# Feed-forward products turned round, and the last part's eight block products replaced by seven

## The chip, the cores and the metric

The kernel runs on one core of a Trainium2 chip. The metric is the device time of one execution in microseconds (us); the median of three runs before is 516.29 us (516.12 to 516.65).

## What is computed

The program has three stages. Banded attention with a few global keys and a distance bias (4 batches, 8 heads, 768 positions, head width 64) gives x of 3,072 tokens by 512. A soft mixture of eight experts with 32 slots follows. Its output, still 3,072 by 512, goes through a dense feed-forward layer, which is what the change touches:

```
h = x @ w_in            # (3072 x 512) @ (512 x 2048)
r = np.maximum(h, 0.0)
g = r * r
return g @ w_out        # (3072 x 2048) @ (2048 x 512)
```

All inputs arrive as 64-bit numbers, or in words from which the kernel makes 32-bit floats itself.

## The kernel before

Every engine runs its instructions in the order in which the program issues them: the schedule is written by hand. The kernel's first part (attention, routing, experts) ends near 220 us in the profile. Since the mixture's output is a product of rank 32 (combine weights `cst` times slot outputs), w_in is first multiplied by the slot outputs into a small matrix `U`, so that one matmul of depth 128 gives h for 128 features and 512 tokens (`gemm1`, L1017).

The 2,048 features are cut into five parts, `WIDTHS` (L32). For each part q and each chunk d of 512 tokens, `gemm1` makes J = width/128 tiles of h. `gate` (L1006) turns each into g: ScalarE (ACT) takes the ReLU out of PSUM (L1008), VectorE (DVE) makes the square in full precision (L1009), ACT the square rounded to the format that TensorE multiplies quickly (L1010), and GpSimd (POOL) the remainder, full minus rounded (L1011; in part 0 DVE does it). w_out is split in the same way into a rounded part `hi` and a remainder `lo` (`conv_out`, L961).

`gemm2` (L1031) takes 128 tokens at a time: g's tile is the stationary operand, 512 columns of w_out the moving one, and for each of the J tiles there are three products, hi by hi, hi by lo, lo by hi (L1042 to L1044), summed in one PSUM bank (tag `acc`, 3 banks). In part 0 ACT copies the bank to the running sum `oacc` (L1049), in the others DVE adds it (L1051); in the last part the sum then goes out by DMA from the SP queue. The very last 128 tokens are done in two halves of 256 columns, the second DMA going from ACT's queue (L1054 to L1061).

The main loop (L1139 to L1154) runs over parts and chunks. `gemm1` and `gate` run one chunk ahead of `gemm2`; the tiles of g have two buffers. Beside them, spread over the first five of the six chunks of a part, `background` (L1129) prepares the next part: it loads the words, converts them to floats (`convert`, L926: one ACT and three DVE operations for 512 columns), makes U (`make_u`, L977) and splits w_out (L971 on ACT, L972 on POOL).

Of the kernel before, what the change touches and what calls it, by code (L numbers as in the profile page):

```python
# [39 lines left out]
def attention_moe_ffn(ctx: ExitStack, tc, qk, vx, nn, phi, w1, w2, w_in, w_out, consts, relw, out):  # L40
    nc = tc.nc
    V, G = nc.vector, nc.gpsimd
# [17 lines left out]
    acc = full("acc", [P, DM])  # L60
# [135 lines left out]
    def slot(tag, shape, dt, name):  # L196
        return (pre if tag[0] == "p" else stream).tile(shape, dt, tag=tag, name=name)
# [752 lines left out]
    def conv_in(q):  # L950
        W = WIDTHS[q]
        if q:
            f = slot("p4", [P, 4, W], F32, f"winf{q}").rearrange("p a c -> p (a c)")
        else:
            f = hZ[:, E * HS : E * HS + 4 * W]
        wq[q] = {"f": f.rearrange("p (a c) -> p a c", c=W)}
        for c0 in range(0, 4 * W, 512):
            yield from convert(raw[q][0], c0, f[:, c0 : c0 + 512], f"i{q}")
            yield

    def conv_out(q):  # L961
        J = WIDTHS[q] // P
        t = slot(("s1", "p6")[q % 2], [P, 4096], F32R, f"w{q}")
        w = t[:, 0 : 2 * J * DM].rearrange("p (a j c) -> p a j c", a=2, c=DM)
        hi, lo = w[:, 0, :, :], w[:, 1, :, :]
# [65 lines left out]
    def gemm2(q, k):  # L1031
        g2 = g_of(q, k // 4)
        ghi, glo = g2[:, 0, :, :], g2[:, 1, :, :]
        whi, wlo = wq[q]["hi"], wq[q]["lo"]
        pa = fps.tile([P, 512], F32, tag="acc", name=f"acc{q}_{k}", bufs=3)
        ms = slice(k % 4 * P, k % 4 * P + P)
        J = WIDTHS[q] // P
        o = oacc[k // 4][:, k % 4, :]

        def products(cs):  # L1040
            for j in range(J):
                nc.tensor.matmul(pa[:, cs], lhsT=ghi[:, j, ms], rhs=whi[:, j, cs], start=j == 0, stop=False)  # L1042
                nc.tensor.matmul(pa[:, cs], lhsT=ghi[:, j, ms], rhs=wlo[:, j, cs], start=False, stop=False)  # L1043
                nc.tensor.matmul(pa[:, cs], lhsT=glo[:, j, ms], rhs=whi[:, j, cs], start=False, stop=j == J - 1)  # L1044

        if k < NT // P - 1 or q < len(WIDTHS) - 1:
            products(slice(0, DM))
            if q == 0:
                nc.scalar.copy(o, pa)  # L1049
            else:  # L1050
                V.tensor_tensor(o, pa, o, op=ALU.add)  # L1051
            if q == len(WIDTHS) - 1:
                nc.sync.dma_start(out[k * P : k * P + P, :], o)
        else:  # L1054
            for c, eng in ((0, nc.sync), (TB, nc.scalar)):
                cs = slice(c, c + TB)
                if c:
                    pa = fps.tile([P, 512], F32, tag="acc", name=f"acc{q}_{k}_2", bufs=3)
                products(cs)
                V.tensor_tensor(o[:, cs], pa[:, cs], o[:, cs], op=ALU.add)  # L1060
                eng.dma_start(out[k * P : k * P + P, cs], o[:, cs])  # L1061
# [256 lines left out]
```

## Time and profile before

| | before |
|---|---|
| median of 3 runs | 516.29 us |
| the profiled execution | 516.84 us |
| its span, first to last instruction | 515.0 us |
| PE busy | 507.0 us (98%) |
| PE weight loads busy | 387.7 us (75%) |
| DVE busy | 379.5 us (74%) |
| ACT busy | 306.4 us (59%) |
| POOL busy | 142.2 us (28%) |
| granted TensorE clock | 1.00 |

PE is TensorE's matmuls. Their recorded times overlap, because matmuls are pipelined; what a matmul costs in a packed stretch is the distance from its start to the next start. The feed-forward products run from about 221 us to the end.

### The profile page before, as it was taken

How to read it: one execution, taken by the hardware profiler on the slowest of the kernel's cores; microseconds unless marked ns; L12 is line 12 of the kernel's file. 1: busy time of each engine (PE TensorE's matmuls, PEld its weight loads, DVE VectorE, ACT ScalarE, POOL GpSimd, SP SyncE). 2: the span in 40 equal slices, each digit the busy share in tenths (PEclk: the TensorE clock that was granted, in tenths of full speed). 3: DMA queues.
4: the chain of work that ended last, by engine and by line, in shares of the span. 5: the costliest groups of instructions: out<-in, count | busy, mean ns of one | idle time of the engine just before them, and what ended most of it. 6: DMA issues, size and time to landing. Idle time of an engine off the chain costs nothing.

```text
span 515.0 us, 9799 instructions
## 1 busy us (share of the span) xinstructions
PE 507.0 (98%) x3532; PEld 387.7 (75%) x3532; DVE 379.5 (74%) x925; ACT 306.4 (59%) x804; POOL 142.2 (28%) x125
## 2 busy tenths in 40 slices
PE   9999999999999999999999999999999999999997
PEld 6777777677767744477887878878888788888886
DVE  7788878787888836688799986968746668445552
ACT  6977877787888302397965555555544455433440
POOL 7000000000000110001443675436744436534450
PEclk9999999999999999999999999999999999999999
DMA  8789989999994899904404040200300000002333
GB/s 285 255 291 301 352 308 329 325 328 301 317 326 153 266 371 423 404 13 165 163 1 163 1 164 1 104 19 1 122 2 0 1 0 3 0 14 110 122 123 122
DMA packets 25975, 86.93 MB, mean 169 GB/s; under 512 B 2882, under 2 KB 5442, under 8 KB 23746
## 3 DMA queue, kind: packets, MB, share of 16 engines
q1 hardware_dynamic: 25776, 86.13, 46.8%
q8 instruction: 29, 0.48, 0.4%
q14 instruction: 24, 0.20, 0.1%
q10 hardware_dynamic: 146, 0.13, 0.1%
HBM read 79.95 MB, written 6.29 MB: 167 GB/s over the span
## 4 chain that ended last, share of the span: by engine, by line
PE 58%; DVE 3%; POOL 0%; issue 0%; ACT 0%; POOLq 0%; DVEq 0%
PE acc L1044 16%; PE acc L1042 16%; PE acc L1043 16%; PE h L1017 4%; PE pSO L922 3%; DVE cvyo L933 1%; PE pu L982 1%; PE pre L818 1%; DVE rg L1009 1%; DVE cvyo L936 1%; DVE cvyo L932 1%; DVE oacc_p L1051 0%; PE pc L883 0%; PE pu L1112 0%; PE sel L912 0%; PE pu L990 0%
## 5 line engine op out<-in xcount | busy, mean ns | idle before, releaser
L1044 PE MATMUL acc<-w,g 128*128 128x512 f32 (+1 forms) x387 | 150.3, 388 | 1.1 <-POOL g L1011 1.1
L1042 PE MATMUL acc<-w,g 128*128 128x512 f32 (+1 forms) x387 | 150.1, 388 | 0.0
L1043 PE MATMUL acc<-w,g 128*128 128x512 f32 (+1 forms) x387 | 150.0, 388 | 0.0
L1011 POOL TENSOR_TENSOR g<-rg,g 128x512 fp32r<-128x512 f32 x84 | 109.0, 1300 | 126.5 <-DVE rg L1009 82.4
L1008 ACT ACTIVATE rg<-h 128x512 f32<-128x512 f32 (+1 forms) x97 | 57.6, 593 | 90.7 <-PE h L1017 84.7
L262 ACT ACTIVATE sm<-sm,nm 128x256 f32<-128x256 f32 (+1 forms) x192 | 92.7, 487 | 1.2 <-DVE nm L247 1.2
L1044 PEld LDWEIGHTS acc<-w,g 128*128 128x128 f32 x387 | 72.7, 188 | 16.8 <-POOL g L1011 1.5
L1042 PEld LDWEIGHTS acc<-w,g 128*128 128x128 f32 x387 | 72.7, 188 | 15.1 <-ACT oacc_p L1049 0.2
L1043 PEld LDWEIGHTS acc<-w,g 128*128 128x128 f32 x387 | 72.7, 188 | 14.9
L1009 DVE SCALAR_TENSOR_TENSOR rg<-h,rg 128x512 f32<-128x512 f32 (+1 forms) x97 | 66.1, 681 | 14.0 <-ACT rg L1008 13.7
L1051 DVE TENSOR_TENSOR oacc_p<-acc,oacc_p 128x512 f32<-128x512 f32 x63 | 43.3, 688 | 44.5 <-PE acc L1044 44.4
L247 DVE CUSTOM_DVE_ANT_0 sm<-s,mask 128x256 f32<-128x256 f32 (+1 forms) x192 | 66.8, 396 | 2.0 <-ACT sm L262 1.2
L1010 ACT ACTIVATE g<-rg 128x512 fp32r<-128x512 f32 (+1 forms) x97 | 61.0, 629 | 3.1
L234 PE MATMUL s<-raw 64*128 64x256 f32 (+1 forms) x384 | 52.8, 397 | 0.0
L273 PE MATMUL pt<-con,sm 128*128 128x128 f32 x352 | 45.4, 276 | 1.6 <-ACT pT L279 1.6
L672 POOL TENSOR_TENSOR lh<-lh 128x256 f32<-128x256 f32 x1 | 0.7, 731 | 158.2 <-PE pt L273 158.2
L290 PE MATMUL o<-pT,v 128*64 128x128 f32 x704 | 44.2, 276 | 0.0
L273 PEld LDWEIGHTS pt<-con,sm 128*128 128x128 f32 x352 | 38.5, 141 | 7.2 <-ACT pT L279 2.8
L234 PEld LDWEIGHTS s<-raw 64*128 64x128 f32 x384 | 32.1, 194 | 14.7 <-DMA v<-in_vx 6.5
L290 PEld LDWEIGHTS o<-pT,v 128*64 128x64 f32 x704 | 37.9, 137 | 6.9 <-ACT sm L262 2.1
L1017 PE MATMUL h<-cu 128*128 128x512 f32 x94 | 37.1, 394 | 0.0
L262 ACT ACTIVATION_READ_ACCUMULATOR sm<-sm,nm 128x1 f32 x192 | 36.9, 192 | 0.0
(222 smaller groups left out, 549.2 us busy)
## 6 DMA issues: line engine op xcount, KB each, us to landing
w<-in_w SPq DMA_DIRECT2D x40, 512.0 KB, 6.6
raw<-in_qk SPq DMA_DIRECT2D x32, 384.0 KB, 4.8
w<-in_w SPq DMA_DIRECT2D x5, 2048.0 KB, 9.2
v<-in_vx SPq DMA_DIRECT2D x32, 256.0 KB, 4.0
raw<-in_qk SPq DMA_DIRECT2D x16, 320.0 KB, 5.0
win<-in_w_in SPq DMA_DIRECT2D x2, 2048.0 KB, 7.9
wout<-in_w_out SPq DMA_DIRECT2D x2, 2048.0 KB, 8.0
out_x<-oacc_p SPq DMA_DIRECT2D x15, 256.0 KB, 2.0
```

Of the source, the lines that this page charges most:

```text
L234: nc.tensor.matmul(sc[hh][:, tt, 0:n, :], lhsT=r[r0 : r0 + D, tt, :], rhs=rhs, start=True, stop=True)
L247: V.tensor_tensor_reduce(out=sm[:, j, 0:n, :], in0=sc[hh][:, tt, 0:n, :], in1=m[:, 2:3, :] if n == 1 else m[:, 0:2, :], scale=-QK_SCALE, s ...
L262: nc.scalar.activation(sm[:, j, 0:n, :], sm[:, j, 0:n, :], AF.Exp, bias=nm[:, j : j + 1], scale=-1.0, accum_out=chunk_sums(i // NPR)[:, tt ...
L273: nc.tensor.transpose(pp[tt][:, hh, c, :], sm[:, 2 * tt + hh, c, :], ident)
L290: nc.tensor.matmul(o[hh * D : hh * D + D, tt, :], lhsT=v[:, c * 3 if tt == 0 else 1 + c, hh * D : hh * D + D], rhs=pT[:, 2 * tt + hh, c, : ...
L1009: V.scalar_tensor_tensor(g, ph, 0.0, r, op0=ALU.max, op1=ALU.mult)
L1010: nc.scalar.activation(g2[:, 0, js, cs], r, AF.Square)
L1011: (G if q else V).tensor_tensor(g2[:, 1, js, cs], g, g2[:, 0, js, cs].bitcast(F32), op=ALU.subtract)
L1017: nc.tensor.matmul(ph, lhsT=wq[q]["U"][:, j * P : j * P + P], rhs=cst[:, d * 2 * TB : d * 2 * TB + 2 * TB], start=True, stop=True)
L1042: nc.tensor.matmul(pa[:, cs], lhsT=ghi[:, j, ms], rhs=whi[:, j, cs], start=j == 0, stop=False)
L1043: nc.tensor.matmul(pa[:, cs], lhsT=ghi[:, j, ms], rhs=wlo[:, j, cs], start=False, stop=False)
L1044: nc.tensor.matmul(pa[:, cs], lhsT=glo[:, j, ms], rhs=whi[:, j, cs], start=False, stop=j == J - 1)
```

## The change

Three things are changed.

First, the second product is turned round in all parts: the weights are now stationary and 512 tokens of g move, so that the sum and the output are transposed (512 features by 3,072 tokens). The host turns the result back. A group is now one of four blocks of 128 output features for a chunk of 512 tokens. Within a group the products with g's rounded part come first, those with its remainder last, and in parts 1 and up the first group's remainder products are held until the second group's rounded ones are issued. The first chunk of part 0 is done in two halves of 256 tokens (`gemm2_first`).

Second, the parts are now 256, 384, 384, 512 and 512 wide. In parts 1 and 2 ACT makes the full square for all tiles but the first (`own`), and in part 0 DVE copies one bank of four. The PSUM banks are regrouped: tags `h` and `k` with two each in place of `h` with four.

Third, the last part is multiplied by Strassen's scheme in Winograd's form. Three times, a pair of 512-token chunks and two blocks of 256 features make a 2x2 block matrix of g; w_out's 512 features by 512 outputs make the other. Seven block products (P1 to P7) take the place of eight. The weights' operands (sums and differences, each split into rounded part and remainder) are made once, in the background of part 3 (`conv_last`, 7 steps of ACT copy and POOL remainder, 4 DVE sums). The operands of g are made for each pair in `y_make`, in seven steps: two ReLUs of 512 and a square of 1,024 elements on ACT for each of the four blocks, four differences t1 to t4 on DVE, a rounded copy on ACT for each of the seven, and a remainder on POOL for five and on DVE for two (P5, P7). A step is issued after every second group of `pair`; a pair's first four steps come during the pair before (for pair 0 during part 3's last chunk). Each product is accumulated in PSUM on top of earlier ones where the scheme allows it, and DVE adds the bank's state to one block of `oacc` after every group: 14 adds a pair. P6, for one, accumulates on P1's bank once DVE has read it.

```diff
-WIDTHS = [256, 384, 512, 512, 384]
+WIDTHS = [256, 384, 384, 512, 512]
+QL = len(WIDTHS) - 1
...
+    def conv_last():
+        wf = raw["f"]
+        for j in range(4):
+            yield from convert(raw[QL][1], j * DM, wf[:, j, :], f"o{QL}")
+            yield
...
+        def operand(n, name, x):
+            hi, lo = (t[n // 4][:, n % 4, a] for a in range(2))
+            nc.scalar.copy(hi, x)
+            yield
+            G.tensor_tensor(lo, x, hi.bitcast(F32), op=ALU.subtract)
...
-        V.scalar_tensor_tensor(g, ph, 0.0, r, op0=ALU.max, op1=ALU.mult)
+        if own:
+            nc.scalar.activation(g, r, AF.Square)
+        else:
+            V.scalar_tensor_tensor(g, ph, 0.0, r, op0=ALU.max, op1=ALU.mult)
...
+    def gemm2_hi(q, d, m):
+        pa = fps.tile([P, 512], F32, tag="acc", name=f"acc{q}_{d}_{m}", bufs=3)
+        for j in range(WIDTHS[q] // P):
+            nc.tensor.matmul(pa, lhsT=whi[:, j, ms], rhs=ghi[:, j, :], start=j == 0, stop=False)
+            nc.tensor.matmul(pa, lhsT=wlo[:, j, ms], rhs=ghi[:, j, :], start=False, stop=False)
+        return pa
+    def gemm2_lo(pa, q, d, m):
+        for j in range(J):
+            nc.tensor.matmul(pa, lhsT=whi[:, j, ms], rhs=glo[:, j, :], start=False, stop=j == J - 1)
+        if q == 0:
+            (V.tensor_copy if m == 3 else nc.scalar.copy)(o, pa)
+        else:
+            V.tensor_tensor(o, pa, o, op=ALU.add)
+    def gemm2(q, d, m):
+        if m == 0 and q:
+            held[0] = gemm2_hi(q, d, 0)
+            return
+        pa = gemm2_hi(q, d, m)
+        if m == 1 and q:
+            gemm2_lo(held[0], q, d, 0)
+        gemm2_lo(pa, q, d, m)
...
+    def y_split(name, y, r, eng):
+        if r is None:
+            nc.scalar.copy(hi, y)
+        else:
+            nc.scalar.activation(hi, r, AF.Square)
+        eng.tensor_tensor(lo, y, hi.bitcast(F32), op=ALU.subtract)
+    def y_block(name, k, half, chunk):
+        for jj in range(2):
+            ph = fps.tile([P, 2 * TB], F32, tag="h", name=f"h{name}_{chunk}_{jj}", bufs=2)
+            nc.tensor.matmul(ph, lhsT=wq[QL]["U"][...], rhs=cst[...], start=True, stop=True)
+            nc.scalar.activation(r[:, jj], ph, AF.Relu)
+        nc.scalar.activation(y, r, AF.Square)
+    def y_make(p):
+        a, b = 2 * p, 2 * p + 1
+        y11, r = y_block("y11", 0, 0, a)
+        y_split("P1", y11, r, G)
+        yield
+        y12, _ = y_block("y12", 1, 0, b)
+        t1 = y_diff("t1", 2, y12, y11)
+        y_split("P5", t1, None, V)
+        yield
+        y22, r = y_block("y22", 3, 1, b)
+        t2 = y_diff("t2", 0, y22, t1)
+        y_split("P6", t2, None, G)
+        yield
+        y_split("P3", y22, r, G)
+        yield
+        t3 = y_diff("t3", 2, y22, y12)
+        y_split("P7", t3, None, V)
+        yield
+        y21, r = y_block("y21", 1, 1, a)
+        y_split("P2", y21, r, G)
+        yield
+        t4 = y_diff("t4", 3, y21, t2)
+        y_split("P4", t4, None, G)
+        yield
+    def pair(p, make):
+        def add(pa, half, chunk, db, cs, done, eng):
+            V.tensor_tensor(o, pa[:, cs], o, op=ALU.add)
+            if done:
+                eng.dma_start(out[...], o)
...
+            for j in range(2):
+                nc.tensor.matmul(pa[:, cs], lhsT=whi[:, j, c], rhs=yhi[:, j, cs], start=new and j == 0, stop=False, **grown)
+                nc.tensor.matmul(pa[:, cs], lhsT=wlo[:, j, c], rhs=yhi[:, j, cs], start=False, stop=False, **grown)
+            for j in range(2):
+                nc.tensor.matmul(pa[:, cs], lhsT=whi[:, j, c], rhs=ylo[:, j, cs], start=False, stop=j == 1, **grown)
+            add(pa, half, chunk, db, cs, done, nc.scalar if n else nc.sync)
+        names = [(n, db) for n in ("P1", "P5", "P6", "P3", "P7") for db in range(2)]
+        last = p == ND // 2 - 1
+        names += [("P2", 0), ("P4", 0), ("P4", 1), ("P2", 1)] if last else [("P2", 0), ("P2", 1), ("P4", 0), ("P4", 1)]
+        for g, (n, db) in enumerate(names):
+            if last and g == len(names) - 1:
+                for c in range(2):
+                    group(n, db, slice(c * TB, c * TB + TB), c)
+            else:
+                group(n, db)
+            if g % 2 == 0:
+                if g == 6:
+                    make = y_make(p + 1) if not last else iter(())
+                next(make, None)
...
+            if ahead[i]:
+                gemm1(*ahead[i], m)
+            else:
+                next(make)
+            if i:
+                gemm2(q, d, m)
+            else:
+                next(first_products, None)
+    for p in range(ND // 2):
+        make = pair(p, make)
```

## Rows read from the trace of the kernel before

**Rows 1.** The page: busy time by engine, and the chain by engine and line.
```profile
PE 507.0 (98%) x3532; PEld 387.7 (75%) x3532; DVE 379.5 (74%) x925; ACT 306.4 (59%) x804; POOL 142.2 (28%) x125
...
PE 58%; DVE 3%; POOL 0%; issue 0%; ACT 0%; POOLq 0%; DVEq 0%
PE acc L1044 16%; PE acc L1042 16%; PE acc L1043 16%; PE h L1017 4%; PE pSO L922 3%; DVE cvyo L933 1%; PE pu L982 1%; PE pre L818 1%; DVE rg L1009 1%; DVE cvyo L936 1%; DVE cvyo L932 1%; DVE oacc_p L1051 0%; PE pc L883 0%; PE pu L1112 0%; PE sel L912 0%; PE pu L990 0%
```
**Rows 2.** Windows of 13 us: length, busy PE, PEld, DVE, ACT, POOL, clock, DMA.
```profile
280.00:293.00 13.00, 13.00 (x59) 10.78 (x58) 12.54 (x18) 8.43 (x15) 6.62 (x6) 1.00 0.00 0
293.00:306.00 13.00, 11.93 (x53) 9.53 (x52) 12.03 (x16) 6.24 (x11) 8.77 (x8) 1.00 0.35 124
```
**Rows 3.** PE in order of time at its gap; waits from 270 us (total, times, longest).
```profile
298.64 0.50 PE L1044 MATMUL acc<-w,g 128*128 128x512 f32 x1 [1.07 <-POOL g L1011]
...
DVE oacc_p L1051 <- PE acc L1044: 44.4, 45, 2.0
```
**Rows 4.** PE in order of time near the end: start, us, line.
```profile
502.77 0.39 PE L1043 MATMUL acc<-w,g 128*128 128x512 f32 x1
...
509.12 0.39 PE L1044 MATMUL acc<-w,g 128*128 128x512 f32 x1
509.35 0.28 PE L1042 MATMUL acc<-w,g 128*128 128x256 f32 x1
...
511.38 0.28 PE L1044 MATMUL acc<-w,g 128*128 128x256 f32 x1
```
**Rows 5.** All engines in order of time, behind the last product.
```profile
511.70 0.42 DVE L1060 TENSOR_TENSOR oacc_p<-acc,oacc_p 128x256 f32<-128x256 f32 x1 [0.65 <-PE acc L1044]
512.15 0.38 ACTq L1061 DMA_DIRECT2D out_x<-oacc_p  x1
```
**Rows 6.** Groups by form, 270 us to the end: busy us, mean ns, idle before.
```profile
L1011 POOL TENSOR_TENSOR g<-rg,g 128x512 fp32r<-128x512 f32 x78 | 101.2, 1299 | 118.0 <-DVE rg L1009 78.4 <-ACT w L971 15.5 <-PE acc L1044 7.5
...
L1010 ACT ACTIVATE g<-rg 128x512 fp32r<-128x512 f32 x77 | 48.7, 633 | 2.5
...
L1051 DVE TENSOR_TENSOR oacc_p<-acc,oacc_p 128x512 f32<-128x512 f32 x63 | 43.3, 688 | 44.5 <-PE acc L1044 44.4
```
**Rows 7.** Groups by form, whole span: other widths on DVE, ACT and POOL.
```profile
L803 DVE TENSOR_TENSOR c_tok<-c_tok,rm 128x768 f32<-128x768 f32 x1 | 1.0, 959 | 0.0
...
L804 ACT ACTIVATE c_tok<-c_tok 128x768 f32<-128x768 f32 x1 | 0.8, 843 | 1.9 <-DVE c_tok L803 1.9
...
L672 POOL TENSOR_TENSOR lh<-lh 128x256 f32<-128x256 f32 x1 | 0.7, 731 | 158.2 <-PE pt L273 158.2
```
**Rows 8.** ACT, POOL and DVE in order of time, 285 to 292 us.
```profile
285.23 0.62 ACT L971 CAST w<-cvyo 128x512 fp32r<-128x512 f32 x1 [1.32 <-DVE cvyo L936]
...
285.97 1.30 POOL L1011 TENSOR_TENSOR g<-rg,g 128x512 fp32r<-128x512 f32 x1 [1.32 <-ACT w L971]
...
290.37 0.68 DVE L1009 SCALAR_TENSOR_TENSOR rg<-h,rg 128x512 f32<-128x512 f32 x1
...
290.97 0.67 DVE L1051 TENSOR_TENSOR oacc_p<-acc,oacc_p 128x512 f32<-128x512 f32 x1
291.01 0.59 ACT L1008 ACTIVATE rg<-h 128x512 f32<-128x512 f32 x1
...
291.63 0.69 DVE L1009 SCALAR_TENSOR_TENSOR rg<-h,rg 128x512 f32<-128x512 f32 x1
```
**Rows 9.** POOL and DVE in order of time near 261 us.
```profile
261.05 1.29 POOL L1011 TENSOR_TENSOR g<-rg,g 128x512 fp32r<-128x512 f32 x1 [1.86 <-PE h L1017]
...
261.39 1.50 DVE L936 SCALAR_TENSOR_TENSOR winf<-cvxi,cvyi 128x512 int32<-128x512 int32 x1
```
**Rows 10.** Groups by form, 270 us to the end: the conversion's DVE operations.
```profile
L933 DVE SCALAR_TENSOR_TENSOR cvyo<-wout,cvyo 128x512 int32<-128x512 int32 x11 | 13.4, 1221 | 0.4
L936 DVE SCALAR_TENSOR_TENSOR cvyo<-cvxo,cvyo 128x512 int32<-128x512 int32 x11 | 12.0, 1089 | 0.4
...
L932 DVE TENSOR_SCALAR cvyo<-wout 128x512 int32<-128x512 int32 x11 | 8.4, 764 | 0.0
```

More of the change, by code (lines that the diff above doesn't have):

```diff
@@ L995, in make_u @@
         wq[q]["U"] = U
+    hk = (t for _ in range(NT) for t in "hk")
     gbuf = {}
@@ L1029, in gemm1_first @@
             gate(0, g_of(0, 0), slice(k0, k1), cs, ph[:, k0:k1, :], rg[:, :, k0:k1, :])
-    def gemm2(q, k):
-        g2 = g_of(q, k // 4)
-        ghi, glo = g2[:, 0, :, :], g2[:, 1, :, :]
+    def gemm2_hi(q, d, m):
+        ghi = g_of(q, d)[:, 0, :, :]
         whi, wlo = wq[q]["hi"], wq[q]["lo"]
-        pa = fps.tile([P, 512], F32, tag="acc", name=f"acc{q}_{k}", bufs=3)
-        ms = slice(k % 4 * P, k % 4 * P + P)
-        J = WIDTHS[q] // P
[L1038 to L1049, printed above, removed]
-            else:
[L1051 to L1061, printed above, removed]
@@ new lines, in gemm2, with region @@
+    def gemm2(q, d, m):
[6 more added lines that the diff above has]
+        gemm2_lo(pa, q, d, m)
+    held = [None]
+    yop, yt = {}, {}
+    PLACE = {"P1": 0, "P5": 1, "P6": 2, "P3": 3, "P7": 4, "P2": 5, "P4": 6}
+    def region(name, k):
+        if "t" not in yt:
+            yt["t"] = slot("p4", [P, 4, 2, 2 * TB], F32, "yt")
+        yt[name] = yt["t"][:, k]
+        return yt[name]
@@ new lines, in y_block @@
+    def y_block(name, k, half, chunk):
+        r = ex.tile([P, 2, 2 * TB], F32, tag="e", name=f"r{name}_{chunk}", bufs=2)
+        for jj in range(2):
+            j = 2 * half + jj
+            ph = fps.tile([P, 2 * TB], F32, tag="h", name=f"h{name}_{chunk}_{jj}", bufs=2)
+            nc.tensor.matmul(ph, lhsT=wq[QL]["U"][:, j * P : j * P + P], rhs=cst[:, chunk * 2 * TB : chunk * 2 * TB + 2 * TB], start=True, stop=True)
+            nc.scalar.activation(r[:, jj], ph, AF.Relu)
+        y = region(name, k)
+        nc.scalar.activation(y, r, AF.Square)
+        return y, r
@@ new lines, in pair, with group @@
+    def pair(p, make):
+        a, b = 2 * p, 2 * p + 1
+        A, Bk = {}, {}
+        def add(pa, half, chunk, db, cs, done, eng):
+            m = 2 * half + db
+            o = oacc[chunk][:, m, cs]
+            V.tensor_tensor(o, pa[:, cs], o, op=ALU.add)
+            if done:
+                eng.dma_start(out[m * P : m * P + P, chunk * 2 * TB + cs.start : chunk * 2 * TB + cs.stop], o)
+        def group(name, db, cs=slice(0, 2 * TB), n=0):
+            if name in ("P1", "P6", "P7", "P4"):
+                bank_, key, tag, nb = A, db, "acc", 3
+            else:
+                bank_, key, tag, nb = Bk, (db, name == "P2", n), "k", 2
+            new = key not in bank_
+            if new:
+                bank_[key] = fps.tile([P, 512], F32, tag=tag, name=f"b{p}{name}{db}{n}", bufs=nb)
+            pa = bank_[key]
+            (whi, wlo), (yhi, ylo) = xop[name], yop[name]
+            c = slice(db * P, db * P + P)
+            grown = {} if new else {"skip_group_check": True}
+            for j in range(2):
[3 more added lines that the diff above has]
+                nc.tensor.matmul(pa[:, cs], lhsT=whi[:, j, c], rhs=ylo[:, j, cs], start=False, stop=j == 1, **grown)
+            half, chunk, done = {"P1": (0, a, False), "P5": (1, b, False), "P6": (0, b, False), "P3": (0, b, True),
+                                 "P7": (1, b, True), "P2": (0, a, True), "P4": (1, a, True)}[name]
+            add(pa, half, chunk, db, cs, done, nc.scalar if n else nc.sync)
[12 more added lines that the diff above has]
+                next(make, None)
+        return make
@@ new lines, in gemm2_first @@
+    def gemm2_first():
+        whi, wlo = wq[0]["hi"], wq[0]["lo"]
+        g2 = g_of(0, 0)
+        pa = [fps.tile([P, 512], F32, tag="acc" if m < 3 else next(hk), name=f"acc0_0_{m}", bufs=3 if m < 3 else 2) for m in range(4)]
+        for n in range(2):
+            cs = slice(n * TB, n * TB + TB)
+            for m in range(4):
+                ms = slice(m * P, m * P + P)
+                for j in range(2):
+                    nc.tensor.matmul(pa[m][:, cs], lhsT=whi[:, j, ms], rhs=g2[:, 0, j, cs], start=n == 0 and j == 0, stop=False)
+                    nc.tensor.matmul(pa[m][:, cs], lhsT=wlo[:, j, ms], rhs=g2[:, 0, j, cs], start=False, stop=False)
+                    nc.tensor.matmul(pa[m][:, cs], lhsT=whi[:, j, ms], rhs=g2[:, 1, j, cs], start=False, stop=n == 1 and j == 1)
+                if n:
+                    nc.scalar.copy(oacc[0][:, m, :], pa[m])
+                if m % 2:
+                    yield
@@ L1135, in background @@
         yield from make_u(q)
+        if q == QL:
+            yield from conv_last()
+            return
         for c in conv_out(q):
             yield from c
-    ahead = [(q, d) for q in range(len(WIDTHS)) for d in range(ND)][1:] + [None]
-    for i in range(len(WIDTHS) * ND):
+    ahead = [(q, d) for q in range(QL) for d in range(ND)][1:] + [None]
+    make = y_make(0)
+    first_products = gemm2_first()
+    for i in range(QL * ND):
         q, d = i // ND, i % ND
-        if d == 0 and q + 1 < len(WIDTHS):
+        if d == 0:
             bg = background(q + 1)
-            total, room = 5 * (WIDTHS[q + 1] // P) + 7, 4 * (ND - 1) - 1
+            total, room = 5 * (WIDTHS[q + 1] // P) + (17 if q + 1 == QL else 7), 4 * (ND - 1) - 1
         for m in range(4):
@@ L1148, in attention_moe_ffn @@
                 next(bg, None)
-            if ahead[i] and ahead[i][1] == 0:
+            if d == ND - 1:
                 for _ in bg:
```

54 lines of the change are left out of this document (46 added, 8 removed).

## Prediction

> **What bounds the kernel now.** I read the page's first lines and its chain of waits, then the feed-forward stretch by windows, then TensorE's order of time, then the durations of the operations that the change multiplies. TensorE (PE) is busy 98% of the span [rows 1]. The chain that ended last runs through PE for 58%, nearly all of it the three products of each block (L1042 to L1044) and the h product (L1017). In the windows PE fills all of its 13 us in every whole stretch but one (the rows give a full one and that one), and the granted clock is 1.00 throughout; DVE is at 12.5 of 13 in the first of them, where the operands of a 512-feature part are prepared [rows 2]. The one gap is 1.07 us at 298.64, where a product waited for POOL's remainder [rows 3]. So this stage pays for each matmul, at the spacing of their starts: from 502.77 to 509.12 there are 28 steps, 0.2268 us each at 512 columns; from 509.35 to 511.38 there are 17, 0.1194 us each at 256 [rows 4]. The durations of 0.39 us overlap and aren't used. Behind the last product stand an add of 0.42 us from 511.70 and the last output DMA, issued at 512.15 [rows 5].
>
> **What is removed.** The last part has J=4 after the change, and J=4 parts pay 4 x 24 x 3 = 288 products over the 3,072 tokens. Seven block products are 7 x 2 halves x 6 matmuls = 84 a pair of token chunks, 252 for the three pairs. The other parts keep their sum of J, 12, so 36 matmuls go: 36 x 0.2268 = **-8.16 us**. The h products stay (8 a pair). Turning the product round (weights stationary, tokens moving) changes neither count nor shape.
>
> **Small terms.** The first chunk's 24 products become 48 of 256 columns: 48 x 0.1194 - 24 x 0.2268 = +0.29. The split at the end costs 12 x 0.1194 - 6 x 0.2268 = 0.07 in place of 18 x 0.1194 - 9 x 0.2268 = 0.11: -0.04. Add and last DMA behind it keep their form: 0. Together **+0.25**.
>
> **Parts 0 to 3.** The 1.07 us gap should go: part 1 now prepares a part of 384 rather than 512 features, the remainder's products come last in a group and those of the first group are held back behind the second's, and ScalarE (ACT) squares in DVE's place. Against that, part 3's background gets three more ACT copies, three more POOL remainders and four DVE sums of 128x512 (some 0.63, 1.30 and 0.69 us each [rows 6]: 1.9, 3.9 and 2.8 us). They lie beside 68 us of products. DVE then has, in each 11.8 us chunk, 8 gates and adds (5.5) and a fifth of eight conversions (0.76 + 1.22 + 1.09 each [rows 10]), four sums and U (5.8 together): 11.3, nearly full. But 45 of 63 adds now wait for PE, that is, DVE is mostly early [rows 3, 6]. Holding the first group leaves its add about 2.7 us before its bank is wanted, a little less cover than now. Bounds -1.1 to +2; I take **-0.5**.
>
> **The new wait: operands made beside the products.** A pair of chunks now costs PE 84 + 8 = 92 starts, 20.9 us, in place of 104, 23.6 us. In that time the operands of the next pair must be made, twice as wide as any operation of this stage today. From the rows at 512 and 768 elements [rows 6, 7], 1,024 come to 1.05 us on ACT (0.63, then 0.84) and 1.23 on DVE (0.69, then 0.96). POOL takes 0.73 for 256 and 1.30 for 512, so 2.43. A pair asks of ACT 8 ReLUs and 11 wide operations, 8 x 0.6 + 11 x 1.0 = 15.8 us at the spacing of starts; of DVE 14 adds (0.6 apart) and 6 wide operations (1.13 apart), 15.2 [rows 8]; of POOL 5 x 2.4 = 12. Each fits, and if only sums counted the wait would be 0.
>
> But DVE and POOL can't overlap here. In [rows 9] a DVE operation with both inputs in SBUF begins when POOL is done: POOL ran from 261.05 to 262.34, DVE's started at 261.39 and took 1.50 instead of 0.69. The adds, with one input in PSUM, aren't slowed (0.69 in the mean of all 63 [rows 6]). The six wide DVE operations have both inputs in SBUF, so they share one resource with POOL: 6 x 1.13 + 12 = 18.8 of 20.9 us. And all engines run in program order, with ACT waiting for DVE's differences t1 to t4, DVE for ACT's rounded copy.
>
> I laid one making out by hand, from ACT's first ReLU at 0, hand-overs at 0.03 (ACT 291.01 + 0.59, DVE at 291.63 [rows 8]). y11 and its copy to 3.0 on ACT. y12 at 5.2; t1 waits for POOL (P1's remainder, 3.2 to 5.4) and is there at 6.7; copy 7.8, P5's remainder on DVE to 8.9. y22 at 9.8; two adds, t2 at 11.4; copies for P6 and P3 to 13.3; POOL on P6's from 12.4. Four adds; t3 wants to start at 13.6, starts at 14.7, is there at 16.0; its copy 17.1; P7's remainder waits for POOL (P3's) and leaves DVE at 19.3. y21 at 19.1, copy 20.1, POOL to 22.4. Four adds to 21.7; t4 waits till 22.4, there at 23.7; copy, ACT free at 24.6. The same without waits for POOL ends at 21.5. So a making lasts **21.5 to 24.6 us** against PE's 20.9.
>
> Who waits for that: the add of P1's second half stands on DVE behind t3 and P7's remainder, and P6's second half accumulates in the bank which that add reads. At 24.6 the first making (begun in part 3's last chunk, four steps ahead) makes PE wait 0.4 us there and 0.5 us for a bank in that last chunk; the second ends its add 3.8 us after PE wants the bank, the third 3.7: 8.4 us. At 21.5 the add is done before PE comes: 0. The rows show the wait but not where each operation will meet POOL: t3 misses POOL's pause by 1.2 us in my layout and t4 by 1.6, and in before the remainder's cousins L933 and L936 lose 0.53 and 0.40 us in the mean, a third of a POOL operation, not all of it [rows 10]. I take the middle, a making of 23 us: the add comes at 18.7 of it; the waits are 0.3, 1.4 and 2.1 us: **+3.8**, with 0 and 8.4 as ends.
>
> **Sum.** -8.16 + 0.25 - 0.5 + 3.8 = -4.6 us. On the profiled execution (516.84: span 515.0 and 1.84 around it) that is 512.2; it stood 0.55 above the median, 516.29, so the forecast is **511.7**.
>
> A rule that speaks against the change: the Trainium skill, TensorE: Matmul & The Clock Gate, section "Why this matters for your kernels", says that idle gaps between bursts of matmuls let the array's clock fall back to half. The trace has one gap of 1.07 us, and its window was granted 1.00. By the rule the longer waits worked out above could bring 1.2 GHz; it is the last rival.
>
> **Rivals.**
> 1. *Cover holds.* The makings start eight groups (some 11 us) ahead of their use, and only two of the three run wholly beside this stage. If t3 and t4 find POOL idle, the wait is 0 to 1: 516.29 - 8.4 + 0.5 = **508.4**. Against it: 18.8 of 20.9 us on the shared resource.
> 2. *The gain is eaten.* All waits fall as laid out, a making of 24.6 us; 8.4 us of waits cancel the 8.4 removed: **516.3**. For it: the layout uses measured durations only. Against it: the third-of-an-operation mean.
> 3. *Slower: ACT's chain through DVE sets the pace.* Each making has some twelve hand-overs between ACT and DVE and back; I took 0.03 us, but POOL began 0.12 us after the ACT copy it waited for (285.23 + 0.62, then 285.97 [rows 8]). With 0.1 more in each a making lasts 25.8 and the waits grow by 3 x 1.2: **519.9**. It decides once a making is over 24.7 us, since its waits then pass the 8.4 us that rival 2 just cancels. Against it: the hand-over from ACT to DVE in the same rows.
> 4. *The clock falls* in the waits. No row of this stage shows the lower level; at 1.2 GHz the 512 columns would be spaced some 0.43 us (estimate, from 0.2268 at 2.4 GHz), so the 18 products of three groups cost 18 x 0.2 = 3.6 us more after each of two waits: on rival 2's 516.3, **523.5**.
> That the change doesn't do what it says would be a count other than 252 in the last part; the loops leave no room for it.
>
> **How the numbers follow.** Forecast (510 to 514.5) 0.40; rival 1 0.27; rival 2 0.15; rival 3 0.14; rival 4 0.04. 0.2% is 1.03 us, about what can be told from no change here. Faster: the forecast, rival 1 and a little of rival 2: 0.68; within: 0.12; slower: 0.20. Leaving out the ends of rivals 1 and 3 and all of rival 4 gives 507.8 to 518; the likeliest case alone 510 to 514.5.
>
> **What would show it.** In the last part 252 products in place of 288, at the old spacing. PE's idle time there before the second half of P6, released by DVE's add, once a pair and growing from the first to the second; if it is before P6's or P3's first matmul and released by POOL, the remainders are the limit instead. DVE's t3 and P7's remainder longer than 1.23 us, by a POOL operation that ends with their wait. ACT waiting for t1 to t4. The gap of 298.64 gone. A pair of chunks between 21 and 23 us. I am wrong if PE is packed there (rival 1), if a pair takes 24.5 or more (2, 3), or if the granted clock leaves 1.00.

## Result and the profile after

The changed kernel takes 523.34 us (median of 4 runs, 521.80 to 525.04) where the kernel before took 516.47 in the runs beside it: ratio 1.0131 [1.0096, 1.0166]. It is slower, by 6.9 us, and lies outside the range of the prediction; the forecast was 511.7. The profiled execution took 523.02, its span 521.2.

First the page: busy time by engine, then the shares of the chain by engine.

```profile
PE 504.9 (97%) x3517; PEld 384.2 (74%) x3517; DVE 389.5 (75%) x922; ACT 334.1 (64%) x835; POOL 155.8 (30%) x119
...
PE 43%; DVE 11%; ACT 7%; issue 1%; POOL 0%; ACTq 0%; DVEq 0%
```

Matmuls went, but PE is no longer alone on the chain: 18% of it now lies on DVE and ACT, which had 3% before [rows 1]. The windows show where (13 us each from 415; columns as in [rows 2]).

```profile
415.00:428.00 13.00, 10.25 (x45) 8.12 (x45) 8.68 (x12) 6.86 (x13) 10.38 (x9) 1.00 0.00 1
...
467.00:480.00 13.00, 11.63 (x44) 9.32 (x45) 10.94 (x14) 7.65 (x9) 6.46 (x3) 0.87 0.26 101
480.00:493.00 13.00, 11.28 (x50) 8.87 (x48) 8.05 (x9) 8.43 (x12) 6.48 (x3) 1.00 0.16 61
493.00:506.00 13.00, 11.34 (x42) 8.87 (x43) 10.79 (x12) 6.49 (x8) 4.76 (x2) 0.87 0.27 102
```

Two things are new against the full windows of before: idle PE, once in part 3 and then throughout the last part, and a granted clock of 0.87 in two windows. Yet no engine is full there; DVE's busiest window has 10.94 of 13. So no engine's load is the limit; the waits come from order. PE in order of time shows each one (start, us, line; in brackets the idle time that a releaser ended):

```profile
250.89 0.50 PE L1081 MATMUL acc<-g,w 128*128 128x512 f32 x1 [0.57 <-DVE oacc_p L1093]
...
422.99 0.50 PE L1081 MATMUL acc<-g,w 128*128 128x512 f32 x1 [2.75 <-ACT g L1054]
...
443.49 0.50 PE L1081 MATMUL acc<-g,w 128*128 128x512 f32 x1 [0.49 <-DVE oacc_p L1095]
...
446.34 0.39 PE L1200 MATMUL b0P<-yop,xs 128*128 128x512 f32 x1
...
468.37 0.50 PE L1200 MATMUL b0P<-yop,xp 128*128 128x512 f32 x1 [1.99 <-DVE oacc L1183]
...
469.99 0.63 PE L1200 MATMUL b1P<-yop,xs 128*128 128x512 f32 x1
470.42 0.63 PE L1201 MATMUL b1P<-yop,xs 128*128 128x512 f32 x1
...
493.51 0.70 PE L1200 MATMUL b1P<-yop,xp 128*128 128x512 f32 x1 [2.24 <-DVE oacc_p L1183]
...
496.14 0.63 PE L1200 MATMUL b2P<-yop,xs 128*128 128x512 f32 x1
...
505.20 0.50 PE L1200 MATMUL b2P<-yop,xs 128*128 128x512 f32 x1 [1.15 <-DVE oacc_p L1183]
```

The pairs begin at 446.34, 469.99 and 496.14, 23.65 and 26.15 us apart; packed they would be 20.9. The banks b0P, b1P and b2P belong to pairs 0, 1 and 2; a product's halves are its two blocks of 128 output features. The waits at 468.37 and 493.51 stand before P4's second half, the one at 505.20 before P6's second half. At 469.99 the starts are 0.43 apart instead of 0.2268: the granted clock is at its lower level, 1.2 GHz, for 3.4 us, and so it is again from about 493.6.

DVE, ACT and POOL in order of time show what the three kinds of wait are made of: part 3 first, then the wait at 468.37, then that at 505.20.

```profile
419.64 1.49 DVE L1002 TENSOR_TENSOR xs<-winf 128x512 f32<-128x512 f32 x1
421.16 0.62 ACT L994 CAST xp<-xs 128x512 fp32r<-128x512 f32 x1 [2.09 <-DVE xs L1002]
421.68 0.59 ACT L1049 ACTIVATE rg<-h 128x512 f32<-128x512 f32 x1
422.30 0.63 ACT L1054 ACTIVATE g<-rg 128x512 fp32r<-128x512 f32 x1
...
455.47 2.13 DVE L1148 TENSOR_TENSOR yt<-yt 128x1024 f32<-128x1024 f32 x1
457.63 1.06 ACT L1129 CAST yop<-yt 128x1024 fp32r<-128x1024 f32 x1 [3.66 <-DVE yt L1148]
458.59 1.07 ACT L1141 ACTIVATE ry<-hy 128x512 f32<-128x512 f32 x2
...
463.91 1.47 DVE L1148 TENSOR_TENSOR yt<-yt 128x1024 f32<-128x1024 f32 x1 [3.15 <-ACT yt L1143]
465.41 1.05 ACT L1129 CAST yop<-yt 128x1024 fp32r<-128x1024 f32 x1 [1.53 <-DVE yt L1148]
466.49 1.23 DVE L1132 TENSOR_TENSOR yop<-yt,yop 128x1024 fp32r<-128x1024 f32 x1 [1.11 <-ACT yop L1129]
467.63 1.28 DVE L1183 TENSOR_TENSOR oacc<-b0P,oacc 128x512 f32<-128x512 f32 x2
...
498.71 2.41 POOL L1132 TENSOR_TENSOR yop<-yt,yop 128x1024 fp32r<-128x1024 f32 x1
498.78 3.42 DVE L1148 TENSOR_TENSOR yt<-yt 128x1024 f32<-128x1024 f32 x1
502.23 1.05 ACT L1129 CAST yop<-yt 128x1024 fp32r<-128x1024 f32 x1 [4.99 <-DVE yt L1148]
503.32 1.22 DVE L1132 TENSOR_TENSOR yop<-yt,yop 128x1024 fp32r<-128x1024 f32 x1 [1.12 <-ACT yop L1129]
504.46 2.48 DVE L1183 TENSOR_TENSOR oacc_p<-b2P,oacc_p 128x512 f32<-128x512 f32 x4
```

*Part 3.* ACT's copy of a weights' sum waits 2.09 us for DVE's sum. The ReLU and the square of g stand behind that copy, and PE needs the square: 2.75 us. The other three sums had made ACT wait before it, 8.0 us together (last view below).

*468.37.* DVE waits 3.15 us for y12's square, makes t1, waits 1.11 for ACT's copy, makes P5's remainder, and only then does the add that frees the bank of P4's second half. While it waits DVE is idle, with that add ready behind: PE had done P7's second half by 461.9. The making itself also begins late. Its first ReLU could follow the h products of 456.70, but begins at 458.59, behind ACT's copy of the difference t4 of the making before, and that t4 took 2.13 us beside a POOL remainder that ended at 456.51. From this ReLU the add ends 9.7 us later; had it begun at 457.1, some 0.7 us of the wait would be left (estimate: PE wants the bank at 466.2).

*505.20.* The same order one step later (t3, copy, P7's remainder, add). Here DVE's t3 also stands beside a remainder on POOL: it begins 0.07 us behind it and takes 3.42 us, where 1.22 is its time without.

The last view groups the stretch 436 us to the end by form (busy us, mean ns | idle before), with the wait of ACT for DVE behind it; the very last line has ACT's wait for DVE's weights' sums in part 3.

```profile
L1132 POOL TENSOR_TENSOR yop<-yt,yop 128x1024 fp32r<-128x1024 f32 x15 | 37.9, 2533 | 42.0 <-ACT yop L1129 20.6 <-PE b1P L1203 10.0 <-issue 5.3
...
L1148 DVE TENSOR_TENSOR yt<-yt 128x1024 f32<-128x1024 f32 x12 | 21.6, 1801 | 11.4 <-ACT yt L1143 11.4
...
L1132 DVE TENSOR_TENSOR yop<-yt,yop 128x1024 fp32r<-128x1024 f32 x6 | 9.3, 1557 | 6.7 <-ACT yop L1129 6.7
...
ACT yop L1129 <- DVE yt L1148: 30.3, 12, 5.0
...
ACT xs L994 <- DVE xs L1002: 8.0, 3, 4.4
```

**Ledger.** From the first product's start to the last one's end the feed-forward products ran from 221.06 to 511.66 before (290.6 us) and from 221.19 to 517.82 after (296.6): +6.0. Since 36 products went (-8.16) and the small terms cost 0.25, +13.9 has to be found. A wait is counted here as the distance between two starts less the spacing of 0.2268. In parts 0 to 3 the waits are 0.73, 2.91 and 0.65 us, and that of before (1.23 so counted, 1.07 idle [rows 3]) is gone: +3.1, and 0.5 more between the very first products. In the last part the waits are 0.21 (at 453.81), 2.15, 2.40 and 1.31: 6.1; the starts at the lower clock come another 3.1 late. Together 12.8. Over all its starts the last part stands 10.0 us above the packed spacing, so 0.8 of the 1.1 us left over is spread there.

### The profile page after: what moved, and what is told of

Read it like the earlier page. It is cut to its first block, busy times and chain, and to the rows that moved or that the text cites. A ratio compares the mean times of both kernels' runs of the same rounds, so it can differ in the third digit from the quotient of the medians.

```text
span 521.2 us, 9797 instructions
## 1 busy us (share of the span) xinstructions
PE 504.9 (97%) x3517; PEld 384.2 (74%) x3517; DVE 389.5 (75%) x922; ACT 334.1 (64%) x835; POOL 155.8 (30%) x119
## 4 chain that ended last, share of the span: by engine, by line
PE 43%; DVE 11%; ACT 7%; issue 1%; POOL 0%; ACTq 0%; DVEq 0%
PE acc L1081 9%; PE acc L1090 9%; PE acc L1082 9%; PE pSO L923 3%; DVE yt L1148 3%; PE h L1061 2%; ACT yop L1129 1%; ACT ry L1141 1%; DVE yop L1132 1%; ACT yt L1143 1%; DVE xs L1002 1%; PE b2P L1200 1%; DVE oacc_p L1095 1%; PE b2P L1201 1%; ACT rg L1049 1%
## 5 line engine op out<-in xcount | busy, mean ns | idle before, releaser
L1081 PE MATMUL acc<-g,w 128*128 128x512 f32 x280 | 109.5, 391 | 3.8 <-ACT g L1054 2.8
L1082 PE MATMUL acc<-g,w 128*128 128x512 f32 x280 | 109.0, 389 | 0.0
L1055 POOL TENSOR_TENSOR g<-rg,g 128x512 fp32r<-128x512 f32 x60 | 81.3, 1361 | 77.1 <-DVE rg L1053 28.5
L1090 PE MATMUL acc<-g,w 128*128 128x512 f32 x280 | 75.8, 390 | 0.0
L1049 ACT ACTIVATE rg<-h 128x512 f32<-128x512 f32 (+1 forms) x73 | 43.0, 589 | 38.9 <-PE h L1061 29.2
L1081 PEld LDWEIGHTS acc<-g,w 128*128 128x128 f32 x280 | 52.6, 188 | 16.0 <-ACT g L1054 3.2
L1090 PEld LDWEIGHTS acc<-g,w 128*128 128x128 f32 x280 | 52.5, 188 | 11.3 <-POOL g L1055 0.3
L1082 PEld LDWEIGHTS acc<-g,w 128*128 128x128 f32 x280 | 52.6, 188 | 10.8
L1132 POOL TENSOR_TENSOR yop<-yt,yop 128x1024 fp32r<-128x1024 f32 x15 | 37.9, 2533 | 42.0 <-ACT yop L1129 20.6
L1095 DVE TENSOR_TENSOR oacc_p<-acc,oacc_p 128x512 f32<-128x512 f32 x48 | 32.4, 687 | 23.3 <-PE acc L1090 23.3
L1054 ACT ACTIVATE g<-rg 128x512 fp32r<-128x512 f32 (+1 forms) x73 | 45.4, 622 | 1.6
L1053 DVE SCALAR_TENSOR_TENSOR rg<-h,rg 128x512 f32<-128x512 f32 (+1 forms) x49 | 33.0, 675 | 10.0 <-ACT rg L1049 10.0
```

The costliest lines, as they stand in the source:

```text
L1081: nc.tensor.matmul(pa, lhsT=whi[:, j, ms], rhs=ghi[:, j, :], start=j == 0, stop=False)
L1082: nc.tensor.matmul(pa, lhsT=wlo[:, j, ms], rhs=ghi[:, j, :], start=False, stop=False)
L1090: nc.tensor.matmul(pa, lhsT=whi[:, j, ms], rhs=glo[:, j, :], start=False, stop=j == J - 1)
L1132: eng.tensor_tensor(lo, y, hi.bitcast(F32), op=ALU.subtract)
```

## Experiments

Theory after the result: three orders of issue cost the time, not any load: (a) in the last part, DVE's adds behind its own hand-overs with ACT; (b) there too, DVE operations with both inputs in SBUF meeting POOL's; (c) in part 3, ACT behind DVE's sums; and the clock falls in the long waits. Rivals: the turned product itself costs (other hand-over of g, held groups), POOL's load alone is the cause, or the clock is the cause and the waits follow from it. The first four kernels shared their runs of the kernel before (516.36 us), the other four theirs (516.49).

**The turn alone.** The last part in eight turned products, as the other parts have it; no Strassen.

```diff
-    ahead = [(q, d) for q in range(QL) for d in range(ND)][1:] + [None]
+    ahead = [(q, d) for q in range(QL + 1) for d in range(ND)][1:] + [None]
...
-        if q == QL:
-            yield from conv_last()
-            return
...
-    for p in range(ND // 2):
-        make = pair(p, make)
```

> All of the change but Strassen's scheme: the last part is multiplied in eight block products, turned round like the others, and prepared as the other parts are. Theory (the loss is in the last part and in its preparation): parts 0 to 3 lose their 2.9 us wait at the end of part 3, the last part is packed at 23.6 us a pair; 516.5 to 518, the clock 1.00. Rival (turning the product round, or the new division of work in parts 0 to 2, costs by itself): 519 or more.

Measured: 516.75 us, 1.0003 [0.9994, 1.0013]. The clock is 1.00, and PE's one wait left is 0.70 us at 250.60, for DVE's copy of a bank in part 0; none in part 3 or behind. So turning the product, holding groups and the new widths cost nothing together, and all of the +6.9 belongs to Strassen's part and its preparation.

**Part 3's sums ahead of the copies.** The four sums go to room of their own, each one operand ahead of ACT's copy of it.

```diff
-        s1 = diff("xs1", x21, x22, ALU.add)
+        s1 = diff(0, x21, x22, ALU.add)
+        yield from operand(5, "P2", x12)
+        s2 = diff(1, s1, x11)
         yield from operand(1, "P5", s1)
-        s2 = diff("xs2", s1, x11)
+        s4 = diff(2, x12, s2)
         yield from operand(2, "P6", s2)
...
```

> The changed kernel, but the four sums of w_out's blocks are made on DVE one operand ahead of ACT's copy of them. Theory (in part 3 ACT stands behind DVE's sums, and the gate of the next chunk behind ACT, which is the 2.75 us wait of TensorE at 423 us): that wait goes, 520 to 521, 2.5 us under the changed kernel's 523.3. Rival (ACT is late for want of time in part 3, whatever the order): 523.

Measured: 521.49 us, 1.0102 [1.0085, 1.0119]: 1.85 less than the changed kernel, a little above the range of the theory, and the intervals overlap. The trace is plainer: the wait at 423 is gone, and the first pair begins at 443.25 instead of 446.34, 3.1 us earlier. Part was given back: the last part takes 72.0 us instead of 71.3, with a wait at P6's second half in pair 1, where the changed kernel has none, and none in pair 2, where the changed kernel has one.

```profile
476.95 0.50 PE L1202 MATMUL b1P<-yop,xs 128*128 128x512 f32 x1 [1.12 <-DVE oacc_p L1185]
```

With (a) out of the way the same edit is measured again below.

**The clock held up.** Dummy matmuls (16, 16 and 8) before the three long waits of the last part.

```diff
+                if (n, db) == ("P4", 1) and not last:
+                    warm(16, con, fps.tile([P, 512], F32, tag="u", name=f"idleP4_{p}"))
+                if (n, db) == ("P6", 1) and last:
+                    warm(8, con, fps.tile([P, 512], F32, tag="u", name=f"idleP6_{p}"))
                 group(n, db)
```

> The changed kernel with idle matmuls put where TensorE waits for DVE's add: 16 before P4's second half in pairs 0 and 1, 8 before P6's second half in pair 2. Theory (the two stretches of 3.4 us at 1.2 GHz behind those waits are a cost of their own, some 1.7 us each): the granted clock is 1.00, 3 us less, 519.5 to 521. Rival (the time at the lower clock only delays products that would have waited later anyway): 522.5 to 523.5 with the clock at 1.00.

Measured: 520.81 us, 1.0095 [1.0078, 1.0113], 2.5 below the changed kernel, though here too the intervals overlap; in the profiled execution the whole span is at clock 1.00. The windows that stood at 0.87, and a new wait:

```profile
467.00:480.00 13.00, 11.55 (x51) 8.78 (x50) 11.88 (x14) 6.93 (x8) 7.53 (x3) 1.00 0.26 101
493.00:506.00 13.00, 12.68 (x59) 9.86 (x59) 11.88 (x13) 6.05 (x7) 8.15 (x3) 1.00 0.27 102
...
477.97 0.50 PE L1200 MATMUL b1P<-yop,xs 128*128 128x512 f32 x1 [1.20 <-DVE oacc_p L1183]
```

PE's lost time is still there (the pairs begin 23.5 and 24.8 us apart, and part of PE's busy time is now dummies), so the clock follows from the waits and is not their cause. It is a price on top of them: the last part takes 69.6 us instead of 71.3. The 3.1 us of late starts are gone, and 1.4 were paid in the new wait at P6's second half of pair 1. Of the 2.4 us between the two profiled executions the other 0.7 lie ahead of the last part, where the kernels are the same, and aren't the edit's.

**The steps cut finer.** The makings in 12 steps instead of 7, with copy and remainder issued a step or two behind the difference, so that adds stand between them.

```diff
         y12, _ = y_block("y12", 1, 0, b)
+        yield
         t1 = y_diff("t1", 2, y12, y11)
-        y_split("P5", t1, None, V)
         yield
         y22, r = y_block("y22", 3, 1, b)
+        y_hi("P5", t1)
+        yield
         t2 = y_diff("t2", 0, y22, t1)
...
+            if g in (0, 1, 2, 4, 5, 6) or g >= 8:
                 next(make, None)
```

> The changed kernel with the same operations for g's operands, issued one after each group instead of a whole step after every second group: a difference on DVE is followed by an add before the remainder that needs ACT's copy, so no add stands behind a difference and a remainder and ACT's round trip between them. Theory (TensorE waits for adds queued on DVE behind the operand making): the waits at P6 and P4 fall to under 1 us in all, the clock stays 1.00, a pair takes 21 to 21.7 us; 514 to 516. Rival 1 (POOL and DVE excluding each other set the pace, whatever the order): waits remain in the same places, a pair at 23 us or more, 519 to 523. Rival 2 (ACT's total work sets it): TensorE waits for POOL's remainders or ACT's copies, 518 or more.

Measured: 517.41 us, 1.0024 [1.0014, 1.0034]; 5.9 below the changed kernel, with not one instruction of the makings taken away, but above the 514 to 516 of the theory: the waits left in the last part are 4.1 us, not under 1. PE's waits from 415 us on:

```profile
422.62 0.50 PE L1081 MATMUL acc<-g,w 128*128 128x512 f32 x1 [2.73 <-ACT g L1054]
...
451.92 0.47 PE L1226 MATMUL b0P<-yop,xs 128*128 128x512 f32 x1 [0.68 <-DVE oacc L1209]
...
474.73 0.47 PE L1226 MATMUL b1P<-yop,xs 128*128 128x512 f32 x1 [1.47 <-DVE oacc_p L1209]
...
497.54 0.47 PE L1226 MATMUL b2P<-yop,xs 128*128 128x512 f32 x1 [1.46 <-DVE oacc_p L1209]
```

Both waits at P4's second half are gone with POOL's remainders all in place: they need the order (a). The clock stays at 1.00. What is left in the last part is at P6's first half, whose bank is read by an add that now stands behind t3; part 3's wait is untouched. DVE and POOL in order of time ahead of the first of them:

```profile
443.88 6.21 POOL L1163 TENSOR_TENSOR yop<-yt,yop 128x1024 fp32r<-128x1024 f32 x2 [4.84 <-ACT yop L1158]
...
444.41 3.43 DVE L1163 TENSOR_TENSOR yop<-yt,yop 128x1024 fp32r<-128x1024 f32 x1
...
448.36 2.81 DVE L1150 TENSOR_TENSOR yt<-yt 128x1024 f32<-128x1024 f32 x1
451.10 1.28 DVE L1209 TENSOR_TENSOR oacc<-b0P,oacc 128x512 f32<-128x512 f32 x2
```

Two POOL remainders take 6.21 us instead of 4.8, and two DVE operations 3.43 and 2.81 instead of 1.22: they exclude each other, and the add comes behind. Alone the four take 2 x 2.41 + 2 x 1.22 = 7.3 us, and from 443.88 to 451.17 they took 7.3.

**POOL's remainders left out** for pairs 1 and 2 (`now[0]` is the number of the pair whose operands are being made).

```diff
-        eng.tensor_tensor(lo, y, hi.bitcast(F32), op=ALU.subtract)
+        if not (eng is G and now[0]):
+            eng.tensor_tensor(lo, y, hi.bitcast(F32), op=ALU.subtract)
```

> The changed kernel, but for pairs 1 and 2 POOL makes no remainders (five of seven a pair; the remainders of pair 0 stay in place, so that part of the products is of other data). Its order is untouched. Theory (POOL and DVE exclude each other, and that lengthens DVE's blocks of difference and remainder): DVE's wide operations take 1.23 us each, the making falls to 21 to 22 us, TensorE's waits at P4 and P6 of pairs 1 and 2 fall under 1.5 us in all; 518.5 to 520. Rival (the order alone, a difference, ACT's copy and a remainder ahead of the add, makes the wait): the waits before P4's second half stay at 2.1 to 2.4 us, 521 to 523.

Measured: 518.06 us, 1.0026 [1.0015, 1.0037]; 5.3 below the changed kernel, and a little below the range of the theory. The waits of PE in the last part, and DVE's wide operations by form:

```profile
469.71 0.50 PE L1204 MATMUL b0P<-yop,xp 128*128 128x512 f32 x1 [1.77 <-DVE oacc L1187]
...
491.43 0.50 PE L1204 MATMUL b1P<-yop,xp 128*128 128x512 f32 x1 [0.35 <-DVE oacc_p L1187]
```

```profile
L1149 DVE TENSOR_TENSOR yt<-yt 128x1024 f32<-128x1024 f32 x12 | 15.8, 1318 | 9.7 <-ACT yt L1144 9.7
...
L1133 DVE TENSOR_TENSOR yop<-yt,yop 128x1024 fp32r<-128x1024 f32 x6 | 8.3, 1391 | 6.7 <-ACT yop L1129 6.7
```

The differences fall from 1801 to 1318 ns in the mean. The wait at 505.20 has no counterpart left, and that at 493.51 falls to 0.35, though the order is the old one: they need the meeting with POOL (b) as well. The one at P4's second half of pair 0 stays, 1.77. It doesn't show what the order does alone: the making before it is pair 0's own, which keeps POOL's remainders, and its t4 at 457.05 takes 2.12 us as in the changed kernel. POOL's load by itself isn't the cause: the kernels below keep every remainder.

**Both orders mended.** The finer steps and part 3's sums ahead, in one kernel (the two diffs above).

> The reordered operand making of e4 together with the early sums of e2. Theory (separate causes, gains add): 517.4 - 2.9 = 514 to 515, and the last part's waits are those of e4, 0.8 and 1.6 and 1.6 us before P6. Rival (part 3's wait only hides another one): 516 to 517.

Measured: 513.59 us, 0.9947 [0.9930, 0.9963], a little better than the theory; 3.8 below the finer steps alone, intervals apart, so (c) is shown too. The four sums still take 1.31 us each in the mean (1.36 in the changed kernel), so it is their place in the order, with the room of their own that it needs, and not their length. It is now faster than before, with three waits left at P6's first half (0.84, 1.62 and 1.62 us).

**Placed against POOL.** The same operations; P3's remainder on POOL goes behind P6's, t3 is issued ahead of the copy for P6, P7's remainder later, so that DVE's two-input operations fall into POOL's pauses where an add waits behind them.

```diff
         y_hi("P3", y22, r)
-        y_lo("P3", y22, G)
         yield
-        y_hi("P6", t2)
         y_lo("P5", t1, V)
         yield
-        y_lo("P6", t2, G)
         t3 = y_diff("t3", 2, y22, y12)
+        y_hi("P6", t2)
+        y_lo("P6", t2, G)
         yield
         y_hi("P7", t3)
+        y_lo("P3", y22, G)
...
```

> e6 with the wide operations placed so that DVE's come where POOL has nothing to do: P3's remainder on POOL after P6's, t3 ahead of P6's rounded copy, P7's remainder two groups later, P2's rounded copy behind t4. Theory (what is left before P6 in e4 is DVE's P5 remainder and t3 waiting for POOL): these take 1.2 to 1.5 us, no wait of TensorE over 0.5 us in the last part, 510.5 to 512.5, under the kernel before by 4 us or more. Rival (DVE's total of 15.2 us and its order leave the adds late anyway): 514.

Measured: 509.67 us, 0.9867 [0.9851, 0.9884], again better than the theory. The waits in the last part come down from 4.1 us to 0.7, and 3.9 us were gained: (b) is shown by placement alone. What changed is DVE's remainders, 2269 ns in the mean of the kernel above and 1210 here; its differences meet POOL as before (1702 and 1861).

**Part 0's copies on ACT.** The last wait ahead of part 3 is for a copy that DVE does in part 0 (0.73 us at 250.89 in the changed kernel).

```diff
-            (V.tensor_copy if m == 3 else nc.scalar.copy)(o, pa)
+            nc.scalar.copy(o, pa)
```

> e7 with all four banks of a chunk in part 0 copied by ACT, as before, instead of one by DVE. Theory (the 0.7 us wait of TensorE at 250 us is for DVE's copy): it goes, 0.5 to 0.7 us under e7. Rival (ACT, at 12.4 of 13 us there, is as late): same as e7.

Measured: 508.74 us (508.35 to 509.17), 0.9854 [0.9838, 0.9870]. The point estimate is 0.9 below the kernel above, though the intervals overlap; the wait is gone from the trace. Its page, three windows and two groups by form:

```profile
PE 499.3 (99%) x3517; PEld 382.3 (75%) x3517; DVE 384.4 (76%) x917; ACT 336.2 (66%) x840; POOL 159.7 (32%) x119
```

```profile
441.00:454.00 13.00, 13.00 (x58) 10.51 (x56) 12.65 (x13) 5.75 (x9) 8.54 (x4) 1.00 0.00 0
...
467.00:480.00 13.00, 12.83 (x57) 10.35 (x56) 9.95 (x14) 10.81 (x15) 10.92 (x4) 1.00 0.21 81
480.00:493.00 13.00, 13.00 (x59) 10.76 (x58) 13.00 (x15) 8.35 (x10) 6.56 (x3) 1.00 0.21 82
```

```profile
L1152 DVE TENSOR_TENSOR yt<-yt 128x1024 f32<-128x1024 f32 x12 | 22.3, 1862 | 2.4 <-ACT yt L1147 2.4
...
L1165 DVE TENSOR_TENSOR yop<-yt,yop 128x1024 fp32r<-128x1024 f32 x6 | 7.3, 1211 | 0.0
```

PE is full but for 0.4 us ahead of two h products near 454 and 0.33 at 468.37, at the same counts of matmuls as the changed kernel. DVE's differences still meet POOL (1862 ns), t3 with an add behind it, but that add is late by 0.33 us at most; its remainders don't meet it (1211). The pairs take 21.4, 21.3 and 19.6 us. Against 516.49 the whole is -7.75 us: the removed products (-8.16), the small terms (+0.25) and the lost gap of before (-1.07) make -9.0; of the 1.2 us between, 0.9 are starts above the packed spacing in the last part. This version beats both kernels.

## Why the prediction was wrong

**Right.** The removed work and its price: 36 products at 0.2268 us arrive in full once the order is mended. The turned product at nothing: 1.0003. The durations: ACT's wide copy 1.05 us (estimate 1.05), DVE's 1.22 undisturbed (1.23), POOL's 2.41 (2.43). That DVE's two-input operations and POOL exclude each other [rows 9], and that P6's second half would wait behind t3 and P7's remainder: it does, at 505.20, though in one pair of the three. The Trainium skill, SBUF — State Buffer, section "Who interferes with whom", says that a DVE instruction with two SBUF inputs contends with a GpSimd instruction that reads SBUF; the trace agrees, with 3.42 us against 1.22.

**The step that failed first: "+3.8" for the new wait.** It measured 10.0: 6.1 of waits, 3.1 of clock, 0.8 spread over the starts. The wait that I had forecast, at P6's second half, was 0.21, 0 and 1.31 us in the three pairs, 1.5 in all. I laid out how long a making takes and then asked for one bank only. The same sentence ("the add stands on DVE behind a difference, a hand-over to ACT and a remainder") holds one step earlier too: the add of P7's second half stands behind t1 and P5's remainder, and P4's second half wants its bank. That wait, 2.15 and 2.40 us, was the largest, and the steps in it took what I had laid out: in the trace t1 is there 6.8 us behind the first ReLU, the copy 7.9, the remainder 9.1 (6.7, 7.8 and 8.9 in the layout). That alone is some 0.7 us of wait; the rest is that t4, late beside POOL, held ACT's copy and so the next making's first ReLU, which my layout had too (ACT free at 24.6, where a pair has 20.9) and which I carried to one bank only. I had gone through the adds behind t3 and t4, not all fourteen. Its end of 8.4 also rested on waits alone and left out what a wait does to the clock.

**The step that failed second: "parts 0 to 3: -0.5".** It measured +3.1 in waits and +3.9 over all starts. I priced the four sums as DVE load (2.8 us beside products) and found room. But ACT's copy of each sum is issued ahead of ACT's ReLU and square for g, which PE needs at once, and the later sums stood on DVE behind a square that waited 1.18 us for ACT's ReLU. So ACT waited for all four sums, 10.1 us in all, and PE in the end 2.75, with DVE busy 8.68 of 13 us in that window. A sum took 1.17 to 1.55 us, not the 0.69 I had priced. The sentence that DVE is mostly early was true of the kernel before [rows 3] and is no cover for an engine that waits for DVE's place in the queue. The 0.73 us at 250.89 is the price of the DVE copy in part 0, which I had not priced.

**The clock.** The last rival had 4% and stood only on top of the eaten gain. It happened, for 3.4 us twice, but seven or eight late starts after each wait cost 1.5 to 1.6 us, where the rival took 18 starts and 3.6. Without it the changed kernel measured 520.81, so the loss stands with or without it. The rule of the Trainium skill that the prediction weighed (TensorE: Matmul & The Clock Gate, "Why this matters for your kernels": idle gaps let the clock fall to half) held for the waits at P4's second half, and not for the longer wait of 2.75 us at 422.99.

**The size of rival 3.** "Slower, 519.9" had the right sign for another reason: hand-overs between ACT and DVE did set the pace, not by 0.1 us of latency in each but by ACT's waits for DVE's place in order, 30.3 us in the changed kernel against 18.3 in the last version. What the changed kernel lost is not a limit of the scheme: rival 1, 508.4, is what its instructions give when they are issued in another order, with one copy moved from DVE to ACT (508.74). That the two agree to 0.3 us is in part luck: rival 1 wanted t3 and t4 to find POOL idle, and DVE's differences still meet it there.

Not settled: the last 1.1 us of the ledger, how much of the waits at P4's second half the order would cost without POOL, and which of the two changes in the run without POOL's remainders (fewer POOL reads, or POOL done earlier with its buffers) counts for how much.

## What to carry to other kernels

Where engines run in program order, a load that fits (20.9 us of PE against 15 of DVE and 16 of ACT) says nothing: list each PSUM bank that is used again, find the instruction that frees it, and read what stands ahead of that instruction on its own engine, above all a round trip to another engine. Cut such a round trip into steps, with the frees between, and put the operations that exclude each other (DVE with two SBUF inputs, POOL) where no free stands behind them. And before a change is given up as slower, look whether the removed work is still in the trace as idle time: here 13.9 us of waits and clock hid a gain of 7.9.

## What the runs showed of the hardware

The granted clock fell to 1.2 GHz for 3.4 us behind waits of 1.99 and 2.24 us in the last part, and stayed at 2.4 GHz behind the waits of 1.47 us and less in the finer steps and of 1.77 us at 469.71 without POOL's remainders. Behind the 2.75 us at 422.99 it stayed up in the changed kernel, and behind 2.76 us at 422.94 it fell in the kernel without POOL's remainders: the length of the wait alone doesn't tell. Dummy matmuls in the three waits kept it at 1.00 in the profiled execution (520.63 us); in one of the other three, the longest (522.25), its mean was 0.997.

POOL loses by the meeting too: two remainders that take 2.41 us each alone took 6.21 in a row beside two DVE operations.
